# The last row pair: product 2 moved to the end, into a bank that VectorE has seeded with product 1 and the residual

## The chip, the cores and the metric

The kernel runs on one core of one Trainium2 chip. The metric is the device time of one execution in microseconds, the median of several runs. Engines are named as the profile names them: PE (TensorE matmul), PEld (its weight loads), DVE (VectorE), ACT (ScalarE), POOL (GpSimd), SP (the engine that issues most DMAs).

## What is computed

With x of 2048 tokens by 640 channels in float32, and xn its layer norm over the channels, the output is the input plus an FNet mixing sublayer plus a token-mixing MLP:

```python
xn = _layernorm(x)
a, b = xn @ dft_hid_re.T, xn @ dft_hid_im.T
fnet = dft_seq_re @ a - dft_seq_im @ b
u = gelu(h.T @ w1 + b1)          # h = _layernorm(xn); 1728 hidden features per channel
mixer = (u @ w2 + b2).T          # back to 2048 tokens by 640 channels
out = x + fnet + mixer
```

## The kernel before

All large products are computed in float32 accuracy from two reduced pieces of each operand: a high part, made by ScalarE (`high`, L150), and the rest, made by VectorE (`low`, L153). `three` (L158 to L164) multiplies high by high, high by low and low by high, so one 128x128x320 block costs three matmuls (L161, L162, L164).

Each stage is a 2x2 block product done with seven block products in the manner of Strassen and Winograd, called here P1 to P7. `row_steps` (L851) makes one such set for one pair of 128-row output tiles, as seven steps of the program. The stages run one after another: the DFT along the sequence, the one along the channels ("hid"), the two halves of the first MLP matrix ("up0", "up1") and the two halves of the second ("down0", "down1"). The change touches one set alone, the last: stage "down1", t = 7, for which `base` is given. This set writes output rows t and t + 8 for good. All sets before it add their results to `out` in DRAM with accumulating DMAs (`collect`, L1032); the last set instead loads what stands in `out` so far (`before`, L1128: two loads, the residual), adds it on chip, and writes the finished rows with plain DMAs (`each`, L1122).

In this set nq is 3, so the stationary blocks have 384 columns. P1, P5, P6 and P7 take nine matmuls, and P2, P3 and P4 take eight, because the last 64-row block is stacked with its remainder (`stacked`, L918). Four blocks of a weight matrix are loaded (A11, A21, A22, A12). VectorE forms the sums from them: `first_sum` (L866: s = A21 + A22), s2 (L1002: s = s - A11, the operand of P6), s4 (L1004: A12 = A12 - s, the operand of P3) and s3 (L1003: A21 = A11 - A21, the operand of P7). P2 uses A12 as it was loaded, so s4 in place comes after P2's pieces have been cut from A12. `fourth` (L990) has ScalarE repeat 64 rows of the operand of P3.

The products accumulate in four banks of PSUM, called z, y, w and u. P1, P6 and P7 all add into z, and z is read after each of them (P1, then P1 + P6, then P1 + P6 + P7). P5 and P3 add into y, which is read after each. P2 has w to itself, and P4 has u. A fresh bank is the next of eight in turn (`bank`, L168).

`read(i)` (L922) takes the result of product i out of its bank:

- i = 1: ScalarE copies z to the left half of the upper output tile (L962).
- i = 5 and 6: VectorE adds the residual on the way out (L958).
- i = 2, 3, 7: VectorE adds the bank to what stands in the output tile (L949). After 3 it adds the residual to the upper left tile (L975), after 7 it writes z + residual to the lower left tile (L979).
- i = 4, the last: VectorE adds the bank to the lower left tile in two halves of 160 columns (L954), and each half has its own DMA, the first on SP's queue and the second on ScalarE's.

The order on each engine is the program's order. `turn_of` (L1224) writes step i: loads, `read` of the product before, sums, the high piece of step i + 2 (AHEAD is 2), extras, the low piece of step i + 2, then what is listed in `behind_lo`, then the matmuls of step i. So in the turn of P1, the high and low piece of the third product of the set are cut, and behind the low piece stand the sums that `behind_lo[s0]` lists.

Of the kernel before, what the change touches and what calls it, by code (L numbers as in the profile page):

```python
# [14 lines left out]
P = 128  # L15
# [12 lines left out]
H2 = D // 2  # L28
# [49 lines left out]
def fnet_plus_mixer(  # L78
# [30 lines left out]
    nc = tc.nc  # L109
# [741 lines left out]
    def row_steps(stage, nq, load_piece, at, end, bias=(None, None), base=None, earliest=0, each=None, aside={}, tail=False, stacked=()):  # L851
# [27 lines left out]

        order = (1, 5, 2, 6, 3, 7, 4) if base else (1, 5, 6, 2, 7, 3, 4)

        early = n < D
        loads_of = {-6: ("A11", "A21", "A22"), -4: ("A12",)} if early else {
# [13 lines left out]
            new_bank += (7, 3)  # L899
        if base:  # L900
            bank_of[4] = "u"
            new_bank += (4,)
        of_moving = {1: 0, 2: 1, 3: 2, 5: 3, 7: 4, 4: 5, 6: 6}

        goes_to = {1: (0, 0, True), 5: (1, 1, True), 6: (0, 1, True), 2: (0, 0, False), 7: (1, 1, False),
# [16 lines left out]
        def read(i):  # L922
            def run():
                if i == 1:
                    held["c"] = place[at]()
                row, half, fresh = goes_to[i]
                cols = slice(half * H2, (half + 1) * H2)
                c, b = held["c"][:, row, cols], banks[bank_of[i]][:, :H2]
                if tail and i in (5, 7, 4):

                    def upper():
                        aside[i](row, half, b)
                        if i == 4:
                            end(held["c"])


                    if i == 7:
                        upper()
                    else:
                        extras[s0 + (4 if i == 5 else order.index(i) + 1)].append(upper)  # L940
                    if i == 5:
                        nc.scalar.activation(c, b, AF.Copy)
                    else:
                        nc.vector.tensor_add(c[:TAIL], b[:TAIL], c[:TAIL])
                    return
                if i in aside:
                    aside[i](row, half, b)
                elif not fresh:
                    nc.vector.tensor_add(c, b, c)  # L949
                elif base and i == 4:  # L950

                    for k, queue in enumerate((nc.sync, nc.scalar)):
                        of = slice(k * H2 // 2, (k + 1) * H2 // 2)
                        nc.vector.tensor_add(c[:, of], b[:, of], c[:, of])  # L954
                        each(c, row, half, True, of, queue)
                    return
                elif base and i != 1:
                    nc.vector.tensor_add(c, b, base()[:, row, cols])  # L958
                elif bias[row] is not None:
                    nc.scalar.activation(c, b, AF.Identity, bias=bias[row])  # L960
                else:
                    nc.scalar.activation(c, b, AF.Copy)  # L962
                if tail and i == 6:

                    low_row = held["c"][:, 1, :]
                    nc.vector.tensor_add(low_row[:, H2:], b, low_row[:, H2:])
                    extras[s0 + 3].append(lambda: nc.scalar.activation(low_row[:, :H2], b, AF.Copy))
                    p5 = banks["u"][:TAIL, :H2]
                    behind_lo[s0 + 3].append(lambda: nc.vector.tensor_add(c[:TAIL], p5, c[:TAIL]))
                if each:  # L970
                    each(c, row, half, i in (7, 3, 4))
                if base and i == 3:

                    c11 = held["c"][:, 0, :H2]
                    nc.vector.tensor_add(c11, c11, base()[:, 0, :H2])  # L975
                    each(c11, 0, 0, True)
                if base and i == 7:

                    nc.vector.tensor_add(held["c"][:, 1, :H2], b, base()[:, 1, :H2])  # L979
                if i == 4 and not each:  # L980
                    end(held["c"])
            return run

        if stacked:

            def second_time():
                last = raw["s"][:, n - P :]
                nc.scalar.activation(last[TAIL:], last[:TAIL], AF.Copy)

            def fourth():  # L990

                last = raw["A12"][:, n - P :]
                nc.scalar.activation(last[TAIL:], last[:TAIL], AF.Copy)

            if not base:
                extras[s0 + 1].append(second_time)
        for e, names in loads_of.items():
            loads[max(s0 + e, earliest)].append(lambda names=names: load(*names))
        if n == D or stacked:
# [2 lines left out]
            s2 = lambda: sub(raw["s"], raw["s"], raw["A11"])  # L1002
            s3 = lambda: sub(raw["A21"], raw["A11"], raw["A21"])  # L1003
            s4 = lambda: sub(raw["A12"], raw["A12"], raw["s"])  # L1004
            if base:
                sums_of = {-2: (first_sum,)}
                behind_lo[s0 - 1].append(s2)
                behind_lo[s0].extend((s4, s3))
                behind_lo[s0 + 1].append(fourth)
            elif stacked:  # L1010
                sums_of = {-2: (first_sum,), 2: (s4,)}
                behind_lo[s0 - 1].append(s2)
                extras[s0].append(s3)
            elif s0 == s_hid:

                behind_lo[s0 - 2].append(first_sum)
                sums_of = {0: (s2,), 1: (s3,), 2: (s4,)}
            else:
                sums_of = {-2: (first_sum, s3), 2: (s4,)}
                behind_lo[s0 - 1].append(s2)  # L1020
# [283 lines left out]
```

## Time and profile before

| what | value |
|---|---|
| time, median of 3 runs | 866.65 us (866.47 to 866.7) |
| span of the profiled execution (first to last instruction) | 865.1 us |
| PE busy | 860.7 us (99%) |
| DVE busy | 695.2 us (80%) |
| ACT busy | 523.0 us (60%) |
| granted TensorE clock | 1.000 |
| first matmul of the last set (P1) | at 852.96 us |
| last matmul of the program (P4) | starts 861.61 us, 0.31 us long |

The page gives no time of the profiled execution other than its span; the median of the runs is 1.55 us above that span. The timeline lists instructions by their start, with the duration behind it and, in brackets, how long the engine had been idle and what ended that. Durations overlap: a matmul of 128x320 lasts 0.31 us but the next starts 0.147 us later.

### The profile page before, as it was taken

The numbers are of one execution on the slowest core, as the hardware profiler recorded it, in microseconds if no ns is written. First come the engines' busy times: TensorE is split into PE (matmuls) and PEld (weight loads), VectorE is DVE, ScalarE is ACT, GpSimd is POOL, SyncE is SP. The second block draws the span as 40 slices with busy tenths as digits, with TensorE's granted clock in tenths as the row PEclk, the third lists the DMA queues.
The fourth block names the chain that finished last, engine by engine and source line by source line (L and its number), as shares of the span: only waits on it lengthen the run. The fifth ranks groups of instructions, "written<-read, shape, count | busy, mean of one in ns | idle before, by whom it ended". The sixth has DMA issues, their size and how long they took to land.

```text
span 865.1 us, 13904 instructions
## 1 busy us (share of the span) xinstructions
PE 860.7 (99%) x4899; PEld 789.6 (91%) x4899; DVE 695.2 (80%) x1177; ACT 523.0 (60%) x968; POOL 158.8 (18%) x215
## 2 busy tenths in 40 slices
PE   9999999999999999999999999999999999999998
PEld 6888888888888888889999999999999999999998
DVE  7898868758767888677877788888679978987887
ACT  5765576763555555547565556676667866555654
POOL 2222131210020211122110101111312221101211
PEclk9999999999999999999999999999999999999999
DMA  9949596695382746869576766665687689766776
GB/s 337 366 103 268 186 245 235 160 292 151 94 191 29 199 102 135 212 107 200 125 167 157 163 138 196 189 173 162 142 185 176 146 241 244 183 141 126 157 170 149
DMA packets 90293, 154.44 MB, mean 179 GB/s; under 512 B 9008, under 2 KB 37424, under 8 KB 89968
## 3 DMA queue, kind: packets, MB, share of 16 engines
q0 software_dynamic: 25008, 57.52, 36.1%
q1 hardware_dynamic: 64928, 95.80, 34.0%
q8 instruction: 38, 0.62, 0.3%
q10 hardware_dynamic: 288, 0.25, 0.1%
q14 instruction: 31, 0.25, 0.1%
HBM read 99.96 MB, written 58.82 MB: 184 GB/s over the span
## 4 chain that ended last, share of the span: by engine, by line
PE 99%; DMA 1%; SPq 0%; ACT 0%; DVE 0%; issue 0%; DVEq 0%
PE psum L161 32%; PE psum L162 32%; PE psum L164 31%; PE psum L515 3%; DMA pieces<-in_dft_seq 1%; ACT piece L150 0%; SPq L503 0%; SPq L539 0%; DVE pair L954 0%; DVEq L1300 0%
## 5 line engine op out<-in xcount | busy, mean ns | idle before, releaser
L153 DVE TENSOR_TENSOR piece<-pieces,piece 128x512 fp32r<-128x512 f32 (+4 forms) x496 | 327.2, 660 | 129.8 <-ACT piece L150 125.2
L150 ACT ACTIVATE piece<-pieces 128x512 fp32r<-128x512 f32 (+3 forms) x472 | 295.3, 626 | 224.6 <-PE psum L164 143.0
L161 PE MATMUL psum<-piece,n 128*128 128x512 f32 x540 | 210.3, 389 | 0.0
L164 PE MATMUL psum<-piece,n 128*128 128x512 f32 x540 | 210.3, 389 | 0.0
L162 PE MATMUL psum<-piece,n 128*128 128x512 f32 x540 | 210.3, 389 | 0.0
L162 PE MATMUL psum<-sup,piece 128*128 128x320 f32 x392 | 120.9, 309 | 0.0
L162 PE MATMUL psum<-sdown,piece 128*128 128x320 f32 x392 | 120.9, 309 | 0.0
L161 PE MATMUL psum<-sup,piece 128*128 128x320 f32 x392 | 120.9, 309 | 0.0
L161 PE MATMUL psum<-sdown,piece 128*128 128x320 f32 x392 | 120.9, 309 | 0.0
L162 PEld LDWEIGHTS psum<-piece,n 128*128 128x128 f32 x540 | 101.4, 188 | 21.1
L161 PEld LDWEIGHTS psum<-piece,n 128*128 128x128 f32 x540 | 101.4, 188 | 20.9
L164 PEld LDWEIGHTS psum<-piece,n 128*128 128x128 f32 x540 | 101.4, 188 | 20.9
L156 DVE TENSOR_TENSOR pieces<-pieces 128x512 f32<-128x512 f32 (+3 forms) x142 | 111.9, 793 | 3.0
L164 PE MATMUL psum<-sup,piece 128*128 128x320 f32 x368 | 113.9, 310 | 0.0
L164 PE MATMUL psum<-sdown,piece 128*128 128x320 f32 x368 | 113.9, 310 | 0.0
L492 POOL DMA_DIRECT2D y<-c x65 | 56.0, 898 | 255.2 <-DVE c L691 154.0
L164 PE MATMUL psum<-shid,piece 128*128 128x320 f32 x280 | 86.7, 310 | 0.0
L162 PE MATMUL psum<-shid,piece 128*128 128x320 f32 x280 | 86.7, 309 | 0.0
L161 PE MATMUL psum<-shid,piece 128*128 128x320 f32 x280 | 86.6, 309 | 0.0
L161 PEld LDWEIGHTS psum<-sdown,piece 128*128 128x128 f32 x392 | 73.6, 188 | 0.0
L161 PEld LDWEIGHTS psum<-sup,piece 128*128 128x128 f32 x392 | 73.6, 188 | 0.0
L162 PEld LDWEIGHTS psum<-sup,piece 128*128 128x128 f32 x392 | 73.6, 188 | 0.0
(135 smaller groups left out, 1107.2 us busy)
## 6 DMA issues: line engine op xcount, KB each, us to landing
pieces<-in_dft_seq SPq DMA_DIRECT2D x120, 256.0 KB, 5.4
y<-c POOLq DMA_DIRECT2D x105, 256.0 KB, 4.9
pieces<-in_w SPq DMA_DIRECT2D x88, 256.0 KB, 3.8
out<-pair POOLq DMA_DIRECT2D x36, 320.0 KB, 5.5
pieces<-y SPq DMA_DIRECT2D x32, 320.0 KB, 4.2
pieces<-in_w SPq DMA_DIRECT2D x32, 192.0 KB, 2.6
out<-in_x SPq DMA_DIRECT2D x16, 320.0 KB, 8.8
up<-pair POOLq DMA_DIRECT2D x8, 640.0 KB, 3.2
```

The source lines that it names most:

```text
L150: nc.scalar.activation(hi, src, AF.Copy)
L153: nc.vector.tensor_sub(lo, src, hi.bitcast(F32))
L156: nc.vector.tensor_sub(to, a, b)
L161: nc.tensor.matmul(psum, wh, mh, start=first, stop=False, skip_group_check=True)
L162: nc.tensor.matmul(psum, wh, ml, start=False, stop=last and wl is None, skip_group_check=True)
L164: nc.tensor.matmul(psum, wl, mh, start=False, stop=last, skip_group_check=True)
L492: nc.gpsimd.dma_start(y_part[m][c][:, j, :], t, accum_op=ALU.add)
L515: nc.tensor.matmul(banks[m, j], channels(k, j)[rows], w[cols], start=n == 0 and k == begin, stop=n == 2 and k == end, skip_group_check=True,)
```

## The change

Only the set with `base` is changed. The order of its products becomes 1, 5, 6, 3, 7, 4, 2 instead of 1, 5, 2, 6, 3, 7, 4. The read of P1 is no longer a copy by ScalarE to the output tile: VectorE adds bank z and the residual and writes the sum into a fresh bank of PSUM, which becomes w. P2, now the last product, accumulates into w without clearing it. At the end VectorE copies the left 160 columns of w out and ScalarE the right 160; each half goes out with its own DMA, on SP's and ScalarE's queue as before. P4 is read whole, and stored with one DMA. Since A12 must stay as it is until the pieces of P2 are cut, s4 writes to a slot of its own (S4), and `fourth` works on S4.

```diff
-        order = (1, 5, 2, 6, 3, 7, 4) if base else (1, 5, 6, 2, 7, 3, 4)
+        order = (1, 5, 6, 3, 7, 4, 2) if base else (1, 5, 6, 2, 7, 3, 4)
...
         if base:
             bank_of[4] = "u"
-            new_bank += (4,)
+            new_bank = (1, 5, 4)
+            operand[3] = "S4"
...
+                if base and i == 1:
+                    banks["w"] = bank()
+                    nc.vector.tensor_add(banks["w"][:, :H2], b, base()[:, row, cols])
+                    return
+                if base and i == 2:
+                    for k, (queue, copy) in enumerate(((nc.sync, nc.vector.tensor_copy), (nc.scalar, high))):
+                        of = slice(k * H2 // 2, (k + 1) * H2 // 2)
+                        copy(c[:, of], b[:, of])
+                        each(c, row, half, True, of, queue)
+                    return
                 if i in aside:
                     aside[i](row, half, b)
-                elif not fresh:
+                elif not fresh or base and i == 4:
                     nc.vector.tensor_add(c, b, c)
-                elif base and i == 4:
-
-                    for k, queue in enumerate((nc.sync, nc.scalar)):
-                        of = slice(k * H2 // 2, (k + 1) * H2 // 2)
-                        nc.vector.tensor_add(c[:, of], b[:, of], c[:, of])
-                        each(c, row, half, True, of, queue)
-                    return
-                elif base and i != 1:
+                elif base:
                     nc.vector.tensor_add(c, b, base()[:, row, cols])
...
-                if base and i == 3:
-
-                    c11 = held["c"][:, 0, :H2]
-                    nc.vector.tensor_add(c11, c11, base()[:, 0, :H2])
-                    each(c11, 0, 0, True)
...
+            def s4_apart():
+                raw["S4"] = raw_slot(n)
+                sub(raw["S4"], raw["A12"], raw["s"])
+
             if base:
                 sums_of = {-2: (first_sum,)}
                 behind_lo[s0 - 1].append(s2)
-                behind_lo[s0].extend((s4, s3))
-                behind_lo[s0 + 1].append(fourth)
+                behind_lo[s0].extend((s4_apart, fourth, s3))
```

The engines' rows below are the program's order around the two places that change. A name such as psum7_103 is a bank, piece_8205 the pieces of the third product of the set, and the brackets name the engines and DMA queues whose semaphores the row waits for.

First place, VectorE, from the low piece of P5 on, before. The row of L156 behind it is s2, the next two are P2's low piece (in two parts), then come s4 and s3, P6's low piece and the read of P5.

```order
L153 TENSOR_TENSOR piece_8190<-pieces0_123,piece_8190 128x384 [waits Activation_49]
L156 TENSOR_TENSOR pieces0_123<-pieces0_123 128x384 [waits DVE_49]
L153 TENSOR_TENSOR piece_8205<-pieces0_123,piece_8205 64x128 [waits DMAHW2_49,PE_49,Activation_49]
L153 TENSOR_TENSOR piece_8205<-pieces0_123,piece_8205 128x256
L156 TENSOR_TENSOR pieces0_123<-pieces0_123 128x384 [waits DVE_49]
L156 TENSOR_TENSOR pieces0_123<-pieces0_123 128x384
L153 TENSOR_TENSOR piece_8222<-pieces0_123,piece_8222 128x384 [waits PE_49,Activation_49]
L958 TENSOR_TENSOR pair_8220<-psum0_96,pair_8144 128x320 [waits DMASW7_49,DMAHW1_49,DMASW0_49,PE_49]
```

The same place on VectorE after the change: s2, P6's low piece, s4 into its own slot, s3, and then the new add from bank z (psum7_103) into w (psum0_96).

```order
L153 TENSOR_TENSOR piece_8190<-pieces0_123,piece_8190 128x384 [waits Activation_49]
L156 TENSOR_TENSOR pieces0_123<-pieces0_123 128x384 [waits DVE_49]
L153 TENSOR_TENSOR piece_8205<-pieces0_123,piece_8205 128x384 [waits PE_49,Activation_49]
L156 TENSOR_TENSOR pieces0_123<-pieces0_123 128x384 [waits DMAHW2_49]
L156 TENSOR_TENSOR pieces0_123<-pieces0_123 128x384
L949 TENSOR_TENSOR psum0_96<-psum7_103,pair_8144 128x320 [waits DMAHW0_49,PE_49]
L153 TENSOR_TENSOR piece_8222<-pieces0_123,piece_8222 64x128 [waits DVE_49,Activation_49]
L153 TENSOR_TENSOR piece_8222<-pieces0_123,piece_8222 128x256
L962 TENSOR_TENSOR pair_8220<-psum1_97,pair_8144 128x320 [waits DMASW7_49,DMAHW1_49,DMASW0_49,PE_49]
```

The low piece of the third product now needs s2's result, and the read of P1, which VectorE did not do before, stands behind it and behind both sums.

The same place on PE before: the last matmul of P5 and the first of the third product, P2, in a bank of its own.

```order
L164 MATMUL psum0_96<-sdown12_7108,piece_8190 128x320
L161 MATMUL psum1_97<-sdown10_6694,piece_8205 128x320 [waits Activation_49]
L162 MATMUL psum1_97<-sdown10_6694,piece_8205 128x320
L164 MATMUL psum1_97<-sdown10_6694,piece_8205 128x320 [waits DVE_49]
L161 MATMUL psum1_97<-sdown11_6936,piece_8205 128x320
```

And on PE after: the last matmul of P5, and then P6, which adds into P1's bank.

```order
L164 MATMUL psum1_97<-sdown12_7108,piece_8190 128x320
L161 MATMUL psum7_103<-sdown10_6694,piece_8205 128x320 [waits DVE_49,Activation_49]
L162 MATMUL psum7_103<-sdown10_6694,piece_8205 128x320
L164 MATMUL psum7_103<-sdown10_6694,piece_8205 128x320
L161 MATMUL psum7_103<-sdown11_6936,piece_8205 128x320
```

The wait for VectorE has moved from the third matmul of the product to its first.

Second place, the end of the program: ScalarE after the change, from the high piece of P3 on (before, the list ended with the high piece of P4 and the DMA).

```order
L150 ACTIVATE piece_8222<-pieces0_123 128x384 [waits PE_49,Activation_49]
L150 ACTIVATE piece_8236<-pieces0_123 128x384 [waits DVE_49,PE_49]
L150 ACTIVATE piece_8249<-pieces0_123 128x384 [waits DMAHW7_49,PE_49]
L150 ACTIVATE piece_8263<-pieces0_123 128x384 [waits DVE_49,DMAHW2_49,PE_49,Activation_49]
L150 ACTIVATE pair_8220<-psum0_96 128x160 [waits DMASW7_49,DMASW0_49,DVE_49]
L1127 DMA out<-pair_8220 128x160 [waits DMAHW0_49,Activation_49]
```

ScalarE's own half of the last bank is new; it waits for VectorE and for two old DMAs, and names no wait for PE. VectorE's last row is its half.

```order
L960 TENSOR_TENSOR pair_8220<-psum1_97,pair_8220 128x320 [waits DVE_49,PE_49]
L153 TENSOR_TENSOR piece_8263<-pieces0_123,piece_8263 64x128 [waits Activation_49]
L153 TENSOR_TENSOR piece_8263<-pieces0_123,piece_8263 128x256
L960 TENSOR_TENSOR pair_8220<-psum7_103,pair_8220 128x320 [waits PE_49]
L978 TENSOR_TENSOR pair_8220<-psum7_103,pair_8144 128x320
L960 TENSOR_TENSOR pair_8220<-psum2_98,pair_8220 128x320 [waits DVE_49,PE_49]
L954 COPY pair_8220<-psum0_96 128x160 [waits PE_49]
```

Where two adds in a row stood (L954, 128x160 each, both on VectorE), one copy of 128x160 stands on VectorE and one on ScalarE.

More of the change, by code (lines that the diff above doesn't have):

```diff
@@ L990, in fourth @@
             def fourth():
-                last = raw["A12"][:, n - P :]
+                last = raw["S4" if base else "A12"][:, n - P :]
                 nc.scalar.activation(last[TAIL:], last[:TAIL], AF.Copy)
```

## The prediction

> **What bounds the kernel now.** I read the page's busy times and its chain of work first, since they say whether any engine but PE matters.
>
> ```profile
> span 865.1 us, 13904 instructions
> PE   860.7 (99%) x4899; PEld 789.6 (91%) x4899; DVE 695.2 (80%) x1177; ACT 523.0 (60%) x968; POOL 158.8 (18%) x215
> PE 99%; DMA 1%; SPq 0%; ACT 0%; DVE 0%; issue 0%; DVEq 0%
> ```
>
> PE is the chain from the first microseconds to the last. The change leaves every matmul before the last set alone and neither adds nor drops one in it (P1 to P7 are 60 before and after). So its effect has two parts only: a gap that it opens or closes between matmuls of the last set, and the path behind the last matmul. Next I read the timeline of that set, PE alone: the last two matmuls of P5, the first of the product behind it, and the last two of the program.
>
> ```profile
> 855.30 0.31 PE L162 MATMUL psum<-sdown,piece 128*128 128x320 f32 x1
> 855.45 0.31 PE L164 MATMUL psum<-sdown,piece 128*128 128x320 f32 x1
> 855.60 0.31 PE L161 MATMUL psum<-sdown,piece 128*128 128x320 f32 x1
> ...
> 861.47 0.31 PE L161 MATMUL psum<-sdown,piece 128*128 128x320 f32 x1
> 861.61 0.31 PE L162 MATMUL psum<-sdown,piece 128*128 128x320 f32 x1
> ```
>
> The third product starts one ordinary step of 0.147 us behind the second: no gap. 41 steps lie between 855.60 and 861.61, at 0.147 each, so there is no gap later either. Before the change, the set is bound by PE's rate alone; there is no stall to win back. The last matmul ends at 861.92.
>
> **The first part: who now releases the third product.** It is P6 instead of P2. P2 had a bank of its own; P6 adds into P1's bank, so it must not start until P1 has been read. Before, ScalarE read P1, at once and two products ahead of P6. Now VectorE reads it, and the order shows where: behind s2, the low piece of P6, s4 and s3. That P6's first matmul waits for this very add follows from the waits: the third matmul needs the low piece and names no wait any more, so the wait on VectorE at the first reaches further than the low piece, and the add is the only reader of psum7_103 there. What VectorE and ScalarE do around this point before:
>
> ```profile
> 853.69 0.56 DVE L156 TENSOR_TENSOR pieces<-pieces 128x384 f32<-128x384 f32 x1
> 854.28 0.73 DVE L153 TENSOR_TENSOR piece<-pieces,piece 64x128 fp32r<-64x128 f32 x2
> 854.48 0.44 ACT L962 ACTIVATE pair<-psum 128x320 f32<-128x320 f32 x1 [0.47 <-PE psum L164]
> 855.04 1.03 DVE L156 TENSOR_TENSOR pieces<-pieces 128x384 f32<-128x384 f32 x2
> 855.63 0.31 ACT L993 ACTIVATE pieces<-pieces 64x128 f32<-64x128 f32 x1 [0.30 <-DVE pieces L156]
> 855.97 0.53 ACT L150 ACTIVATE piece<-pieces 128x384 fp32r<-128x384 f32 x1
> 855.99 0.55 DVE L153 TENSOR_TENSOR piece<-pieces,piece 128x384 fp32r<-128x384 f32 x1
> 856.45 0.48 DVE L958 TENSOR_TENSOR pair<-psum,pair 128x320 f32<-128x320 f32 x1
> ```
>
> ScalarE had emptied P1's bank at 854.92. VectorE starts s2 at 853.69; nothing ahead of s2 changes, so that holds after the change as well. What follows is new in this set, but the set before it (t = 6) has exactly this chain, s2, then ScalarE's high piece of P6, then VectorE's low piece:
>
> ```profile
> 844.89 1.03 DVE L156 TENSOR_TENSOR pieces<-pieces 128x384 f32<-128x384 f32 x2
> 845.54 0.53 ACT L150 ACTIVATE piece<-pieces 128x384 fp32r<-128x384 f32 x1 [0.74 <-DVE pieces L156]
> 846.10 0.56 DVE L153 TENSOR_TENSOR piece<-pieces,piece 128x384 fp32r<-128x384 f32 x1 [0.18 <-ACT piece L150]
> ```
>
> From the start of s2 to the start of the low piece are 1.21 us. So the low piece of P6 starts at 853.69 + 1.21 = 854.90. Back to back, 384-column operations follow each other every 0.47 us (two L156 and the next L153: 855.04 to 855.99; L153 to L958: 0.46). So s4 starts at 855.37, s3 at 855.84, and the new add at 856.31. The trace has no VectorE operation that writes PSUM. The nearest rows are the same add with its output in SBUF, 0.48 (L958 above), and from below the 0.40 after which VectorE itself goes on (L949 at 857.61, next row 858.01, quoted further down); from above I double it, 0.97. I take 0.48, the row with the same sources and size: the add ends at 856.79.
>
> Then PE has to be woken. The only waits of PE for another engine lie at the start of the kernel:
>
> ```profile
> 6.54 0.63 ACT L150 ACTIVATE piece<-pieces 128x512 fp32r<-128x512 f32 x1 [1.57 <-DMA pieces<-in_dft_seq]
> 7.23 0.73 PE L515 MATMUL psum<-piece,n 128*128 128x512 f32 x2 [0.27 <-ACT piece L150]
> 7.23 2.12 PE L515 MATMUL psum<-piece,n 128*128 128x512 f32 x8 [0.27 <-ACT piece L150]
> ```
>
> ScalarE ends at 7.17 and PE starts at 7.23: 0.06. The first two matmuls take 0.73, all eight 2.12, so six further steps take 1.39, or 0.23 each, while the first step takes 0.73 - 0.39 = 0.34 (one matmul of that width is 0.39 long): 0.11 more, the weight load that nothing hides. P6 then runs as if its first matmul had started at 856.79 + 0.06 + 0.11 = 856.96, not 855.60: **1.36 us**. P6 waits for two semaphores, one of them in an instruction ahead of the matmul, for which I add 0.04: **1.4 us** lost. From below 1.3 (the add released 0.08 earlier), from above 1.9 (a doubled add).
>
> Is the loss given back or repeated? It can't be given back: behind P6 PE runs at its rate, and 42 matmuls remain. Repeated it could be at P3, which adds into P5's bank and waits for VectorE's read of P5. S4 starts at 855.37; from s4 to the end of the high piece of its product is 1.46 (855.04 to 856.50 above, with L993 between), so ScalarE is done at 856.83 and the two-part low piece starts at 856.86. The rows below show that the next add follows 0.64 later: 857.50 to 857.98. P3 is due at 856.96 + 9 x 0.147 = 858.28. So 0.24 us is spare, after a handoff of 0.06. P7 waits for VectorE's read of P6, which can't begin before P6's last matmul has ended (856.96 + 8 x 0.147 + 0.31 = 858.45) and ends near 859.0; P7 is due at 859.45. P4 and P2 have banks of their own, and their pieces have 0.6 us and more to spare, since the gap lets ScalarE and VectorE catch up. Nothing further is late.
>
> ```profile
> 856.97 0.73 DVE L153 TENSOR_TENSOR piece<-pieces,piece 64x128 fp32r<-64x128 f32 x2
> 857.61 0.48 DVE L949 TENSOR_TENSOR pair<-psum,pair 128x320 f32<-128x320 f32 x1
> 858.01 0.55 DVE L153 TENSOR_TENSOR piece<-pieces,piece 128x384 fp32r<-128x384 f32 x1
> ...
> 860.04 0.48 DVE L975 TENSOR_TENSOR pair<-pair 128x320 f32<-128x320 f32 x1
> ...
> 861.19 0.48 DVE L979 TENSOR_TENSOR pair<-psum,pair 128x320 f32<-128x320 f32 x1
> 861.96 0.56 DVE L954 TENSOR_TENSOR pair<-psum,pair 128x160 f32<-128x160 f32 x2 [0.28 <-PE psum L162]
> 862.55 0.35 ACTq L1124 DMA_DIRECT2D out<-pair  x1
> ```
>
> Costs at nothing: the residual is now wanted at 856.31 instead of 858.48, but its loads were issued at 843.25 and landed 4.8 us later at most:
>
> ```profile
> 843.25 0.84 SPq L1132 DMA_DIRECT2D pair<-out  x2
> DMA to landing us min/median/max: 4.5/4.6/4.8
> ```
>
> The add L975 goes (0.48 on VectorE); it stood beside matmuls, so it is worth nothing. P4's store becomes one DMA, issued when VectorE has read P4, eight matmuls ahead of the end. Before, the store of the tile read after P7 stood at the same distance (L949 at 860.79, P4 behind it also has eight), so SP's queue is as far ahead of the last store as it was.
>
> **The second part: behind the last matmul.** Before, both adds of 160 columns run on VectorE: start at 861.96, 0.04 behind PE's end; the second ends at 862.52, and the DMA of its half, the last, is issued at 862.55, or 0.63 behind PE's end. The change wants the halves side by side. The order says otherwise: ScalarE's copy names no wait for PE, although PE has just filled the bank. It waits for VectorE, and the only row of VectorE that itself waits for the last matmul is the other half's copy. So the halves go one behind the other, now with a handoff between two engines.
>
> ```profile
> L954 DVE TENSOR_TENSOR pair<-psum,pair 128x160 f32<-128x160 f32 x2 | 0.6, 320 | 0.3 <-PE psum L162 0.3
> L878 DVE COPY pieces<-pieces 64x128 f32<-64x128 f32 x8 | 1.8, 224 | 0.3
> L962 ACT ACTIVATE pair<-psum 128x320 f32<-128x320 f32 x97 | 42.2, 435 | 43.8 <-PE psum L164 40.7 <-PE psum L162 2.2
> L988 ACT ACTIVATE pieces<-pieces 64x128 f32<-64x128 f32 x7 | 2.2, 309 | 0.2
> ```
>
> VectorE's copy lies between the small copy, 0.22, and the add of the same size, 0.32; I take 0.29, nearer the add, whose size it has. The handoff to ScalarE is 0.03 (855.04 + 0.56 to 855.63). ScalarE's copy lies between 0.44 (320 columns) and, for 128 columns, 0.31: I take 0.31, the nearer in size, and its DMA follows 0.03 later. So the last DMA goes out at 0.04 + 0.29 + 0.03 + 0.31 + 0.03 = 0.70 behind PE's end instead of 0.63: **0.07 us later** (0.00 to 0.23 by the bounds). What lies behind that DMA is the same transfer and the same end of the program.
>
> The Trainium skill has the rule behind this wait: "PSUM — Partial Sum Buffer", section "PSUM bank collisions raise a hardware error", says that two engines must not access the same bank and quadrant at once, reads against reads included, and that software has to order them. The order's wait agrees; by the rule the halves can't overlap, and without it ScalarE's half would end as early as VectorE's and the term would be about -0.3.
>
> **Sum.** +1.4 + 0.07 = +1.47 us on a span of 865.1, so 866.6. The page has no other time of that execution; the median of the runs is 1.55 above the span, and I add the difference to the median: 866.65 + 1.47 = **868.1 us**, 0.17% slower. A measurement of this kernel can tell about 0.2% (1.73 us) from no change, so this counts as within 0.2%.
>
> **Rivals.**
>
> *A dearer seed.* If the add into PSUM takes longer than the one into SBUF, each tenth goes straight into PE's gap. From +0.26 on, the total passes 1.73 and the change is slower by over 0.2%; with the doubled add it is 866.65 + 1.9 + 0.07 = 868.6. For it: no row shows a write to PSUM. Against it: reading PSUM costs nothing (L979 reads PSUM, L975 reads SBUF alone, 0.48 both).
>
> *The gap costs the clock.* The clock row shows that PE's clock does fall behind its work:
>
> ```profile
> 863.60:864.60 1.00, 0.00 (x0) 0.00 (x0) 0.00 (x0) 0.00 (x0) 0.00 (x0) 1.00 0.14 39
> 864.60:865.10 0.50, 0.00 (x0) 0.00 (x0) 0.00 (x0) 0.00 (x0) 0.00 (x0) 0.53 0.00 0
> ```
>
> The clock (behind the engines' columns) is full up to 864.60, 2.7 us after the last matmul, and 0.53 in the half microsecond behind it. Were the 42 remaining matmuls to run at half, they'd take 6.2 us more: 874.3. My gap is 1.1 us of idle (855.76 to 856.89), less than half of 2.7, so the trace speaks against it. The Trainium skill, "TensorE: Matmul & The Clock Gate", Part 1, has the clock halve after an idle window of about 3.4 us; by that rule, too, this gap is short of it.
>
> *No stall.* If the release of P6 came by 855.60 (the add done 1.3 us earlier than I have it, as when it stood ahead of the low piece in VectorE's row), only the tail would count: 866.65 + 0.07 = 866.7, and with a tail as the change describes it (halves side by side, ScalarE's DMA at 0.04 + 0.31 + 0.03 = 0.38 instead of 0.63) 866.4. That is the other side, faster than before; it decides at an add that ends before 855.5, and VectorE's order, which is fixed, speaks against it. *Halves side by side with the stall* gives 866.65 + 1.4 - 0.25 = 867.8: the change does at the end what it says. The wait in ScalarE's row speaks against it.
>
> **How the numbers follow.** Forecast 0.77 (868.1; 867.9 to 868.35 by its bounds without the doubled add); dearer seed or a second wait at P3 0.13 (868.4 to 868.8); halves side by side 0.04; no stall 0.04; clock 0.02. The range of 867.6 to 868.7 takes in the first three cases. Faster by over 0.2% would need 1.73 us, and the best case above, no stall with the halves side by side, gains 0.25; so 0.02 for what I don't see. Slower by over 0.2%: the dearer seed, the clock and a little of the forecast's upper edge, 0.17. Within 0.2%: 0.81.
>
> **What would show it.** PE's timeline should have one gap, between the end of P5 and a first matmul of P6 near 856.9, released by VectorE's add (L949 of the new kernel) that starts near 856.3; no gap at P3 or P7; the last matmul 1.4 us later relative to the start, and ScalarE's copy of 160 columns starting after VectorE's has ended, not beside it. The prediction is wrong if P6 follows P5 without a gap, if the add's row is not near 0.48, if P3 shows a gap of its own, or if both copies start together.

## The result, and the profile after

The changed kernel takes **868.23 us** (median of 16 runs, 868.1 to 869.73) against 866.65 for the kernel before (16 runs, 866.38 to 868.49). The ratio is 1.0019, 95% interval 1.0012 to 1.0026: 0.19% slower, where 868.1 was forecast. The profiled span grew from 865.1 to 866.5 us.

First the busy times of the page of the kernel after. They say almost nothing: PE still works 860.6 us.

```profile
span 866.5 us, 13903 instructions
PE 860.6 (99%) x4899; PEld 789.3 (91%) x4899; DVE 694.7 (80%) x1176; ACT 522.8 (60%) x968; POOL 158.8 (18%) x215
```

The place shows in PE's timeline of the last set: the last matmul of P5, the first two of P6, and the last one of the program.

```profile
855.23 0.31 PE L164 MATMUL psum<-sdown,piece 128*128 128x320 f32 x1
856.73 0.38 PE L161 MATMUL psum<-sdown,piece 128*128 128x320 f32 x1 [1.19 <-ACT piece L150]
856.95 0.31 PE L162 MATMUL psum<-sdown,piece 128*128 128x320 f32 x1
...
862.81 0.31 PE L162 MATMUL psum<-sdown,piece 128*128 128x320 f32 x1
```

P6 starts 1.495 us behind the last matmul of P5 instead of 0.147, and its second matmul 0.22 behind its first. All other steps are ordinary, so PE loses 1.42 us in all, at this one place. The whole set began 0.22 us earlier in this execution than in the one of before (P1 at 852.74 instead of 852.96); such an offset is not the change's, so from here on times are compared by their distance to P1's start or to PE's end.

VectorE and ScalarE at the same place, from s2 to the read of P5:

```profile
853.47 0.56 DVE L156 TENSOR_TENSOR pieces<-pieces 128x384 f32<-128x384 f32 x1
854.12 0.52 ACT L150 ACTIVATE piece<-pieces 128x384 fp32r<-128x384 f32 x1 [0.74 <-DVE pieces L156]
854.68 0.56 DVE L153 TENSOR_TENSOR piece<-pieces,piece 128x384 fp32r<-128x384 f32 x1 [0.65 <-ACT piece L150]
855.15 1.02 DVE L156 TENSOR_TENSOR pieces<-pieces 128x384 f32<-128x384 f32 x2
855.74 0.31 ACT L992 ACTIVATE pieces<-pieces 64x128 f32<-64x128 f32 x1 [1.09 <-DVE pieces L156]
856.08 0.94 ACT L150 ACTIVATE piece<-pieces 128x384 fp32r<-128x384 f32 x2
856.09 0.49 DVE L949 TENSOR_TENSOR psum<-psum,pair 128x320 f32<-128x320 f32 x1
856.64 0.73 DVE L153 TENSOR_TENSOR piece<-pieces,piece 64x128 fp32r<-64x128 f32 x2
857.28 0.48 DVE L962 TENSOR_TENSOR pair<-psum,pair 128x320 f32<-128x320 f32 x1
```

L949 is the new add: it starts 2.62 us behind s2, ends at 856.58, and P6 follows 0.15 later. The view of waits, which lists who waited for whom, how long and how often, names another releaser:

```profile
PE psum L161 <- ACT piece L150: 1.2, 1, 1.2
```

This is a wait put down to the wrong engine. The L150 that ends at 856.61 (856.08 + 0.52) is the high piece of **P3**, nine matmuls further on. P6 waits on ScalarE for its own high piece, and that was done at 854.64. The first experiment shows which reading is right.

The end of the program after: VectorE's copy, ScalarE's copy, the last DMA.

```profile
863.16 0.33 DVE L954 COPY pair<-psum 128x160 f32<-128x160 f32 x1 [0.68 <-PE psum L162]
863.52 0.30 ACT L150 ACTIVATE pair<-psum 128x160 f32<-128x160 f32 x1 [3.45 <-DVE pair L954]
863.85 0.35 ACTq L1127 DMA_DIRECT2D out<-pair  x1
```

The copies stand one behind the other, 0.03 apart. PE's end is where its last matmul ends (862.81 + 0.31 = 863.12). The last DMA is issued 0.73 us behind it, before 0.62; the span ends 3.39 behind PE's end, before 3.17. So the change costs 1.42 on PE and 0.22 behind it, 1.64 together, of which the medians show 1.58.

### The profile page after: what moved, and what is told of

It reads as the page before. It is cut to its first block, busy times and chain, and to the rows that moved or that the text cites. A ratio compares the mean times of both kernels' runs of the same rounds, so it can differ in the third digit from the quotient of the medians.

```text
span 866.5 us, 13903 instructions
## 1 busy us (share of the span) xinstructions
PE 860.6 (99%) x4899; PEld 789.3 (91%) x4899; DVE 694.7 (80%) x1176; ACT 522.8 (60%) x968; POOL 158.8 (18%) x215
## 4 chain that ended last, share of the span: by engine, by line
PE 98%; DVE 1%; DMA 0%; ACT 0%; issue 0%; SPq 0%; ACTq 0%
PE psum L161 32%; PE psum L162 32%; PE psum L164 31%; PE psum L515 3%; DMA pieces<-in_dft_seq 0%; DVE piece L153 0%; ACT piece L150 0%; DVE pair L960 0%; DVE pieces L156 0%; DVE pieces L874 0%; SPq L539 0%; DVE n L394 0%; DVE pair L954 0%; ACT pieces L992 0%; ACT near L236 0%
## 5 line engine op out<-in xcount | busy, mean ns | idle before, releaser
L150 ACT ACTIVATE piece<-pieces 128x512 fp32r<-128x512 f32 (+3 forms) x472 | 295.3, 626 | 225.2 <-PE psum L164 140.4
L156 DVE TENSOR_TENSOR pieces<-pieces 128x512 f32<-128x512 f32 (+3 forms) x142 | 111.7, 792 | 3.4 <-DMA pieces<-in_dft_seq 0.5
L161 PEld LDWEIGHTS psum<-sdown,piece 128*128 128x128 f32 x392 | 73.6, 188 | 1.4 <-ACT piece L150 1.4
L161 PEld LDWEIGHTS psum<-sup,piece 128*128 128x128 f32 x392 | 73.6, 188 | 0.0
L162 PEld LDWEIGHTS psum<-sdown,piece 128*128 128x128 f32 x392 | 73.6, 188 | 0.0
```

The lines of the kernel that those rows point to most:

```text
L150: nc.scalar.activation(hi, src, AF.Copy)
L156: nc.vector.tensor_sub(to, a, b)
L161: nc.tensor.matmul(psum, wh, mh, start=first, stop=False, skip_group_check=True)
L162: nc.tensor.matmul(psum, wh, ml, start=False, stop=last and wl is None, skip_group_check=True)
```

## The experiments

That PE waits at P6 is seen; what has to be told apart is why. The first theory, called A where the expectations use letters, is that of the **cover**: P2 needs no sum, so in third place its eight matmuls (1.17 us) hid the chain by which VectorE and ScalarE get P6 and P3 ready. Without P2 there, something of that chain is late whatever the details, and curing one link shows the next. Against it stand the edits themselves: that VectorE reads P1, late in its queue; that the sum is written into PSUM; and, at the end, the handoff between two engines. Line numbers differ by a few between kernels. "PE loss" is what the 60 matmuls of the set take beyond 0.147 us a step.

### VectorE reads P1 before it cuts P6's low piece

```diff
+        if i == len(steps) - 7:
+            def low_later():
+                ready[j] = steps[j][1]()
+            sums[i + 1].extend([low_later] + behind_lo.pop(i))
-        if 0 <= j < len(steps):
+        elif 0 <= j < len(steps):
             ready[j] = steps[j][1]()
```

> The changed kernel with VectorE's read of P1 moved ahead of the low piece of P6, so that it stands directly behind s2. Theory A (the loss is cover, not one row): PE's gap in front of P6 goes, but with P2 no longer between P6 and P3, P3 comes due about 1.32 us behind the start of P6, and its chain on VectorE (s4, s3, low piece of P3, read of P5) is as late as before; so the gap moves to P3, 1.2 to 1.35 us long, and the time stays near 868.05 (1.39 us above the kernel before). Theory B (the place of the read of P1 in VectorE's row is the whole cause): no gap anywhere, 866.75, the tail's 0.1 us above the kernel before.

Measured: 868.19 us, ratio 1.002 (1.0011 to 1.0029). In this kernel, VectorE's read of P1, then ScalarE's high pieces from P3's on, and VectorE's low piece of P3 and read of P5:

```profile
854.30 0.50 DVE L949 TENSOR_TENSOR psum<-psum,pair 128x320 f32<-128x320 f32 x1 [0.23 <-PE psum L164]
...
856.13 1.35 ACT L150 ACTIVATE piece<-pieces 128x384 fp32r<-128x384 f32 x3
856.69 0.73 DVE L153 TENSOR_TENSOR piece<-pieces,piece 64x128 fp32r<-64x128 f32 x2 [0.47 <-ACT piece L150]
857.33 0.48 DVE L962 TENSOR_TENSOR pair<-psum,pair 128x320 f32<-128x320 f32 x1
```

Its PE: the end of P5 and the start of P6, then the end of P6 and the start of P3.

```profile
855.28 0.31 PE L164 MATMUL psum<-sdown,piece 128*128 128x320 f32 x1
855.42 0.31 PE L161 MATMUL psum<-sdown,piece 128*128 128x320 f32 x1
...
856.60 0.31 PE L164 MATMUL psum<-sdown,piece 128*128 128x320 f32 x1
857.96 0.38 PE L161 MATMUL psum<-sdown,piece 128*128 128x320 f32 x1 [1.06 <-DVE pair L962]
```

P6 has no gap now, although P3's high piece, the first of the three in the row of L150, ends no earlier than in the kernel after (856.13 + 0.52 = 856.65, or 3.87 behind P1's start in both): so it was VectorE's add that P6 waited for, and the wait view was wrong. But the gap has only moved. P3 adds into P5's bank, whose read stands behind P3's own low piece, and it loses 1.29. In the kernel after this second wait was hidden behind the first with 0.21 to spare (the read ends at 857.76, P3 may start 0.15 later, and was due at 858.12): 1.42 less 0.21 is 1.21, and with the 0.07 of P3's slow second step 1.28.

### The product order alone

The order of the products and S4 stay, and all else is as before the change: ScalarE copies P1, P2 has a bank of its own, VectorE adds at the end.

```diff
-            new_bank = (1, 5, 4)
+            new_bank = (1, 5, 2, 4)
...
-                    banks["w"] = bank()
-                    nc.vector.tensor_add(banks["w"][:, :H2], b, base()[:, row, cols])
+                    nc.scalar.activation(c, b, AF.Copy)
...
-                        copy(c[:, of], b[:, of])
+                        nc.vector.tensor_add(c[:, of], b[:, of], c[:, of])
...
+                if base and i == 3:
+                    c11 = held["c"][:, 0, :H2]
+                    nc.vector.tensor_add(c11, c11, base()[:, 0, :H2])
```

> The changed kernel's product order and its S4 slot, but P1 is read by ScalarE to the output tile as before the change, P2 has a bank of its own, nothing is seeded in PSUM, and the last product is added out in two halves on VectorE as before. Theory A (cover): no gap at P6, a gap of 1.2 to 1.35 us at P3, tail as before the change; 867.9 to 868.0. Theory B (the read of P1 on VectorE is the cause): no gap, 866.65. Theory C (writing the seed to PSUM is what costs): no gap, 866.65.

Measured: 868.21 us, 1.0019 (1.0009 to 1.0028). The loss on PE is 1.63: 1.32 at P6 and 0.31 at P3. No theory had the first. ScalarE shows why, from the repeat of 64 rows (`fourth`) to its read of P1, and PE at P6:

```profile
855.66 0.31 ACT L994 ACTIVATE pieces<-pieces 64x128 f32<-64x128 f32 x1 [1.09 <-DVE pieces L156]
856.03 0.44 ACT L948 ACTIVATE pair<-psum 128x320 f32<-128x320 f32 x1
```

```profile
855.16 0.31 PE L164 MATMUL psum<-sdown,piece 128*128 128x320 f32 x1
856.52 0.41 PE L161 MATMUL psum<-sdown,piece 128*128 128x320 f32 x1 [1.05 <-ACT pair L948]
```

`fourth` now stands in the turn of P1 and waits for s4, and ScalarE's read of P1 is queued behind it. So this kernel had a new obstacle of its own, and didn't yet show what the order costs. The same edit with `fourth` one turn later:

```diff
+        if i == len(steps) - 7:
+            sums[i + 1].append(behind_lo[i].pop(1))
```

> The kernel of order_alone, with ScalarE's repeat of the 64 rows of S4 moved behind its read of P1, since it had stood ahead of it and waited for s4. Theory A (cover): no gap at P6; P3 is held by the chain s4, repeat, high piece, low piece, read of P5, which nothing in this kernel shortens, so one gap of 1.2 to 1.35 us at P3, tail as before the change (last DMA 0.62 us behind PE's end), 867.9 to 868.1. Theory B (VectorE's read of P1): no gap, 866.65.

Measured: 867.92 us, 1.0015 (1.0006 to 1.0024), with a loss of 1.27, all at P3. VectorE's read of P5, then PE at the end of P6 and the start of P3:

```profile
857.26 0.48 DVE L961 TENSOR_TENSOR pair<-psum,pair 128x320 f32<-128x320 f32 x1
856.54 0.31 PE L164 MATMUL psum<-sdown,piece 128*128 128x320 f32 x1
857.89 0.39 PE L161 MATMUL psum<-sdown,piece 128*128 128x320 f32 x1 [1.04 <-DVE pair L961]
```

This kernel has no seed in PSUM, ScalarE reads P1 in good time, and its tail is that of before (0.62 and 3.17 behind PE's end, as there). It is still 1.32 slower. So the order of the products, with VectorE's queue left as it is, is enough to bring the cost: by way of s4, `fourth`, the high and the low piece of P3 and the read of P5. The seed is not needed for it.

### The end of the program on VectorE alone

```diff
-                    for k, (queue, copy) in enumerate(((nc.sync, nc.vector.tensor_copy), (nc.scalar, high))):
+                    for k, (queue, copy) in enumerate(((nc.sync, nc.vector.tensor_copy), (nc.scalar, nc.vector.tensor_copy))):
```

> The changed kernel with both halves of the last bank copied by VectorE, one behind the other, each with its own DMA as now. If ScalarE's half waits for VectorE's half and the handoff and ScalarE's longer start are what the tail pays, the last DMA is issued 0.62 us behind PE's end instead of 0.73 and the time falls by 0.10 us, to about 868.13; the gap at P6 stays at 1.4 us. If the two engines side by side were worth something, it would rise by 0.1 or more.

Measured: 868.09 us, 1.0017 (1.0008 to 1.0026). The two copies and the last DMA of this kernel, whose PE ends at 863.18:

```profile
863.22 0.55 DVE L954 COPY pair<-psum 128x160 f32<-128x160 f32 x2 [0.68 <-PE psum L162]
863.80 0.35 ACTq L1127 DMA_DIRECT2D out<-pair  x1
```

Two copies take 0.55, two adds took 0.56 before. So a copy out of PSUM is no cheaper than an add with PSUM, and the seed, which turns the last add into a copy, buys nothing. The DMA goes out 0.62 behind PE's end, as before. Handing the second half to ScalarE costs 0.11 there, and 0.13 more until the span's end (3.15 here, 3.39 in the kernel after). The medians, 0.14 apart, have overlapping intervals; the profile carries this reading.

### VectorE's queue in another order

VectorE does s2, s4, the read of P1, P6's low piece, s3, the read of P5, P3's low piece: each read ahead of the low piece that stood in its way, and s3 one turn later.

```diff
+        at = i - (len(steps) - 7)
+        if 0 <= at < 3:
+            def low_later():
+                ready[j] = steps[j][1]()
+            sums[i + 1].append(low_later)
+            if at == 0:
+                sums[i + 1].append(behind_lo[i].pop())
-        if 0 <= j < len(steps):
+        elif 0 <= j < len(steps):
             ready[j] = steps[j][1]()
```

> The changed kernel with VectorE's rows rearranged in the last set: s2, s4, read of P1, low piece of P6, s3, read of P5, low piece of P3, read of P6, low piece of P7. Theory A (cover): every release now comes at or just before PE needs it; a gap of 0.0 to 0.25 us is left at P3's third matmul, which waits for the low piece, and the time is 866.75 to 867.0. If the gap came from the seed in PSUM or from the product order as such, it would stay near 1.4 us and 868.2.

Measured: 867.14 us, 1.0005 (0.9997 to 1.0014). VectorE's reads of P1 and P5 and P3's low piece:

```profile
854.58 0.49 DVE L949 TENSOR_TENSOR psum<-psum,pair 128x320 f32<-128x320 f32 x1
...
855.92 0.48 DVE L962 TENSOR_TENSOR pair<-psum,pair 128x320 f32<-128x320 f32 x1
856.43 0.73 DVE L153 TENSOR_TENSOR piece<-pieces,piece 64x128 fp32r<-64x128 f32 x2
```

And PE at the second and third matmul of P3:

```profile
856.88 0.31 PE L162 MATMUL psum<-sdown,piece 128*128 128x320 f32 x1
857.22 0.41 PE L164 MATMUL psum<-sdown,piece 128*128 128x320 f32 x1
```

Both banks come free in time. What is left is the low piece of P3, which ends at 857.16, so that the third matmul of P3 waits: 0.28 us of loss instead of 1.42. The seed is still there, and so is the handoff at the end. It is therefore VectorE's queue that sets how much of the cover is missed. The time is 0.14 above the expected range: the gap is 0.03 longer than its upper bound, and the tail, counted at 0.1, costs 0.21.

### The last bank in one copy, or in two banks

Both build on the kernel above. In the first ScalarE copies all 320 columns, then both DMAs go out. In the second the halves of P2 have banks of their own, so that the two copies may run side by side; its 8 matmuls become 16 of 160 columns.

```diff
-                    for k, (queue, copy) in enumerate(((nc.sync, nc.vector.tensor_copy), (nc.scalar, high))):
+                    high(c, b)
+                    for k, queue in enumerate((nc.sync, nc.scalar)):
                         of = slice(k * H2 // 2, (k + 1) * H2 // 2)
-                        copy(c[:, of], b[:, of])
```

> The kernel of vector_order, with the last bank copied out by one ScalarE operation of 320 columns, and the two half DMAs behind it. The copy should take 0.44 us and both DMAs go out 0.50 to 0.56 us behind PE's end, instead of 0.39 and 0.73; the gap at P3 stays at 0.28. If the later of the two DMAs sets the end, the time falls by 0.15 to 0.2 us against vector_order, to 866.95; if the earlier one counts, it rises by 0.1.

```diff
+                    if base and i == 2:
+                        for k in range(2):
+                            of = slice(k * H2 // 2, (k + 1) * H2 // 2)
+                            three(
+                                banks["w"][k][:, of], (w[0][:, ks], None if q == nq - 1 else w[1][:, ks]),
+                                (m[:, 0, of_moving[i], of], m[:, 1, of_moving[i], of]), False, q == nq - 1,
+                            )
+                        continue
...
-                        copy(c[:, of], b[:, of])
+                        copy(c[:, of], banks["w"][k][:, of])
```

> The kernel of vector_order, with P2 accumulated in two banks, 160 columns each (16 matmuls of 160 columns instead of 8 of 320), seeded by two adds. If the shared bank is what puts ScalarE's half behind VectorE's, both copies now start together, 0.04 us behind PE's end, and the last DMA goes out at 0.40 instead of 0.73. If something else orders them, ScalarE still starts 0.36 later. The 16 matmuls take 1.2 us at best (no more than 8 of 320) and 2.3 us if their pace is that of 320 columns. Time 866.9 to 867.3, or 868 at that worst pace.

One copy: 867.18 us, 1.0007 (0.9998 to 1.0016), no better than two. The copy itself is quick:

```profile
861.98 0.44 ACT L150 ACTIVATE pair<-psum 128x320 f32<-128x320 f32 x1 [3.09 <-PE psum L162]
862.45 0.37 ACTq L1127 DMA_DIRECT2D out<-pair  x1
```

Both DMAs go out 0.50 behind PE's end (861.94), 0.23 ahead of the last one in the kernel above, yet the span ends 3.44 behind PE instead of 3.38. The expected gain is lost behind the issue: the first packet of ScalarE's DMA starts 1.02 us after it instead of 0.87, and SP comes to its last wait 2.44 behind PE's end instead of 2.38. In this execution the two transfers, started together, were slower than two that are 0.34 apart.

Two banks: 867.41 us, 1.001 (1.0001 to 1.0018). One of P2's matmuls, and the copies at the end:

```profile
862.01 0.28 PE L161 MATMUL psum<-sdown,piece 128*128 128x160 f32 x1
862.13 0.27 PE L162 MATMUL psum<-sdown,piece 128*128 128x160 f32 x1
862.21 0.32 DVE L965 COPY pair<-psum 128x160 f32<-128x160 f32 x1 [1.03 <-PE psum L162]
862.44 0.30 ACT L150 ACTIVATE pair<-psum 128x160 f32<-128x160 f32 x1 [3.67 <-PE psum L162]
862.77 0.35 ACTq L1138 DMA_DIRECT2D out<-pair  x1
```

Here the halves do overlap, from 862.44 to 862.53, each as long as alone, and the last DMA goes out 0.37 behind PE's end (862.40). ScalarE's copy now waits for PE and no longer for VectorE. The Trainium skill, "PSUM — Partial Sum Buffer", section "Specifications (TRN2)", says that ScalarE and VectorE reach PSUM in parallel at full rate as long as they don't meet in a bank; these rows agree. The price is on PE: a matmul of half the columns comes every 0.112 us, not every 0.073. From its first matmul (860.49) to PE's end the product takes 1.91 us instead of 1.34. It earns 0.36 at the last DMA against 0.57 on PE, and the time lies 0.11 above the range expected at the better paces.

### s3 on GpSimd

The kernel with VectorE's queue in another order again, with the sum s3 taken off VectorE.

```diff
+            def s3_pool():
+                nc.gpsimd.tensor_sub(raw["A21"], raw["A11"], raw["A21"])
...
-                behind_lo[s0].extend((s4_apart, fourth, s3))
+                behind_lo[s0].extend((s4_apart, fourth, s3_pool))
```

> The kernel of vector_order, with s3 computed by GpSimd, which is idle here, so that VectorE has 0.47 us less to do ahead of the read of P5. Theory A (VectorE's queue sets every release): the gap of 0.28 us at P3 goes (0.00 to 0.1), the time is 866.7 to 866.9, the tail's 0.1 above the kernel before. If GpSimd's sum is late for P7 (more than 2 us long), a gap appears there instead.

Measured: 866.96 us, 1.0005 (0.9996 to 1.0014). The PE loss is 0.11, still at the third matmul of P3. The time is 0.06 above the expected range, again for the tail of 0.22 that was counted at 0.1. P6's low piece on VectorE, GpSimd's sum, and P3's low piece:

```profile
854.80 0.55 DVE L153 TENSOR_TENSOR piece<-pieces,piece 128x384 fp32r<-128x384 f32 x1
854.93 1.30 POOL L1006 TENSOR_TENSOR pieces<-pieces 128x384 f32<-128x384 f32 x1
855.97 0.85 DVE L153 TENSOR_TENSOR piece<-pieces,piece 64x128 fp32r<-64x128 f32 x2
```

P3's low piece takes 0.85 instead of 0.73 while GpSimd works beside it, which is most of what is left. With the tail on VectorE as well (the edit of the third experiment on top):

> The kernel of pool_sum with the tail of tail_vector: both cures together. If gap and tail simply add, the gap at P3 stays near 0.11 us, the span behind PE's end falls from 3.39 to 3.15 us, and the time is 866.6 + 0.1 = 866.65 to 866.8, level with the kernel before. If P2 at the end with a seeded bank has a gain of its own, the time falls below 866.5.

Measured: 866.71 us against 866.64, ratio 1.0001 (0.9992 to 1.001), the loss on PE 0.13, the span's end 3.16 behind PE. The cost of the change is gone, and nothing is gained over the kernel before. The last try puts GpSimd's sum two products earlier, where the expectation had it harmless:

```diff
-                sums_of = {-2: (first_sum,)}
+                sums_of = {-2: (first_sum,), -1: (s3_pool,)}
...
-                behind_lo[s0].extend((s4_apart, fourth, s3_pool))
+                behind_lo[s0].extend((s4_apart, fourth))
```

> As pool_vector_tail, with GpSimd's sum issued one step earlier, ahead of its two stores, so that it runs beside other work of VectorE than the low piece of P3. In pool_sum that low piece took 0.85 us instead of 0.73 while GpSimd's sum ran. If that overlap is the 0.11 us that is left at P3, the gap goes to 0.00 to 0.05 and the time is 866.55 to 866.7; if not, it stays at 0.11 and 866.7. No gain below 866.5 is expected either way, since the copies at the end take as long as the adds did.

Measured: 867.08 us, 1.0005 (0.9996 to 1.0014): a miss, with a PE loss of 0.40, of which 0.30 at P6. VectorE's last low piece before P5's, GpSimd's sum, and VectorE from P5's low piece on:

```profile
852.04 0.56 DVE L153 TENSOR_TENSOR piece<-pieces,piece 128x384 fp32r<-128x384 f32 x1
852.15 1.33 POOL L1006 TENSOR_TENSOR pieces<-pieces 128x384 f32<-128x384 f32 x1 [5.92 <-DVE pieces L878]
852.92 0.98 DVE L153 TENSOR_TENSOR piece<-pieces,piece 128x384 fp32r<-128x384 f32 x1
853.93 1.15 DVE L156 TENSOR_TENSOR pieces<-pieces 128x384 f32<-128x384 f32 x2
```

The low piece of P5 now runs beside the sum and takes 0.98 instead of 0.55; s2 and everything behind it start 0.43 later. The Trainium skill, "SBUF — State Buffer", section "Who interferes with whom", says that a VectorE instruction with two inputs in SBUF and a GpSimd instruction that reads SBUF hold a shared port exclusively, the later one blocked until the other is done. The rows agree: GpSimd's sum ends at 853.48, and the low piece ends 0.42 behind that, about the 0.47 that such an operation occupies VectorE. They agree the other way round too: in both kernels the sum starts about 0.1 behind a low piece of VectorE, and it ends 0.88 behind that piece's end (852.60 to 853.48 here, 855.35 to 856.23 in the first kernel with GpSimd). By the rule, 0.42 to 0.45 of its 1.3 us would be waiting; no run has the sum by itself. By that rule the place of GpSimd's sum has to be one where VectorE reads PSUM or waits, and this chain has little of it.

### All runs together

Each row: time, change of the median against the kernel before on the same chip, PE loss, change of the span's end behind PE, and the sum of the two.

| kernel | time us | change | PE loss | end | sum |
|---|---|---|---|---|---|
| the change | 868.23 | +1.58 | 1.42 (P6) | +0.22 | 1.64 |
| read of P1 first | 868.19 | +1.56 | 1.29 (P3) | +0.21 | 1.50 |
| order alone | 868.21 | +1.58 | 1.63 (P6, P3) | 0.00 | 1.63 |
| order alone, `fourth` later | 867.92 | +1.32 | 1.27 (P3) | 0.00 | 1.27 |
| tail on VectorE | 868.09 | +1.46 | 1.43 (P6) | -0.02 | 1.41 |
| VectorE's queue | 867.14 | +0.51 | 0.28 (P3) | +0.21 | 0.49 |
| one copy | 867.18 | +0.58 | 0.27 (P3) | +0.27 | 0.54 |
| s3 on GpSimd | 866.96 | +0.36 | 0.11 (P3) | +0.22 | 0.33 |
| s3 on GpSimd, tail on VectorE | 866.71 | +0.07 | 0.13 (P3) | -0.01 | 0.12 |
| GpSimd's sum early | 867.08 | +0.44 | 0.40 (P6) | +0.01 | 0.41 |

Two banks stands apart, since its last product has other matmuls: 867.41, +0.81. In every row the two terms give the change to within 0.06 us. That is what lets differences of 0.3 us be read that no interval of the ratios resolves.

## Why the prediction was right, point by point

**The release of P6** held, term by term. The add starts 2.62 us behind s2, exactly as forecast (856.31 less 853.69). It takes 0.49, forecast 0.48: writing PSUM costs nothing over writing SBUF, and the doubled add of the rival is out. PE starts 0.15 behind the add's end instead of 0.10 (of which 0.04 rested on no row), and the slow first step, put down to the exposed weight load, costs 0.07 instead of 0.11: 0.22 for 0.21. That these two cancel is luck. Together 1.42, forecast 1.4.

**No gap at P3** held: 0.21 us was spare, forecast 0.24. But the prediction took this as the end of the matter, and the experiments show that it is half of the cause. The prediction named the place of the add in VectorE's queue as the reason, and its rival without a stall let the loss vanish if the add stood ahead of P6's low piece. That rival's price was wrong: with the add there the kernel is still 1.56 slower, because P3 has a chain of nearly the same length behind it. What costs is that P2, the one product that needs no sum, no longer stands in third place while VectorE's queue stays as it was: with that queue in another order the loss is 0.28, with P2 still last.

**The clock** stayed full through the gap, as said. The margin was smaller than the prediction's 2.7 us, though: in the kernel with two banks the clock had fallen 1.6 us behind the last matmul (last section). The window from 855.70 to 857.10 of the kernel after; the clock stands behind the five engines' columns:

```profile
855.70:857.10 1.40, 0.37 (x3) 0.40 (x3) 1.33 (x5) 1.24 (x3) 0.00 (x0) 1.00 1.21 181
```

**The tail** was right in kind, the halves one behind the other, and short in size: +0.22 where +0.07 was forecast. VectorE's copy took 0.325 instead of 0.29; the nearer row, the add of the same size, was the right one to the last digit, and going below it was the error. ScalarE's copy took 0.30 (forecast 0.31), the handoff 0.03. So the last DMA is 0.105 later, not 0.07. The other 0.12 is behind that DMA, where "the same end of the program" was assumed: from SP's last wait to the end of the span are 1.01 us, before 0.89. In all kernels whose last copy is ScalarE's this stretch is 1.00 to 1.01, and 0.87 to 0.89 in all where VectorE does it. One drain of SP is longer by 0.10; the first row is the kernel after, the second the kernel before (least, median and longest time in ns).

```profile
L1303 SPq DRAIN  x3: 7/7/118, 865.6 to 866.2; - x3
```

```profile
L1300 SPq DRAIN  x3: 7/7/18, 864.3 to 864.8; - x3
```

Why the end of the program depends on who copied last stays open; the runs show only that the two go together. Also open is what the halves would give if they ran side by side in one bank: wherever both engines copied out of one bank here, ScalarE's half waited for VectorE's, so no run shows it.

**The range.** The measured 868.23 lies within the forecast's own bounds of 867.9 to 868.35. The upper one is not the sum of its terms, which is 868.28 (866.65 + 1.4 + 0.23); the terms as measured, 1.42 and 0.22, give 868.29.

## What to carry to other kernels

When a product, a tile or a step is moved, ask what its old place was hiding: here 1.17 us of matmuls that needed no sum covered a chain of sums and pieces on two slower engines, and the profile of before, without any gap, could show that only through who was due when. Curing the first late link isn't a cure until the next one is checked: P6 alone was late by 1.42 us and P3 alone by 1.29, so an experiment on one of them by itself would have shown nothing. And behind the last matmul, price a copy out of PSUM as the add that it replaces, and count a second engine as a second step in line unless it has a bank of its own.

## What the runs showed of the hardware beyond that

- PE follows the engine that it waits for at different distances. The first matmul of a product came 0.15 us behind the end of a VectorE read in the kernel after (856.58 to 856.73), with the read first (857.81 to 857.96) and with the order alone and `fourth` later (857.74 to 857.89), but 0.05 behind ScalarE's read (856.47 to 856.52). The third matmul of P3, whose bank and high piece were ready, came 0.06 behind VectorE's low piece (857.16 to 857.22). So it isn't the engine alone that sets the distance; what does stays open.
- The clock does not fall a fixed time behind the last matmul. Before, it had dropped 2.7 us behind it. After, it is still full in the window that ends 2.9 us behind PE's end:

```profile
865.10:866.00 0.90, 0.00 (x0) 0.00 (x0) 0.00 (x0) 0.00 (x0) 0.00 (x0) 1.00 0.00 0
```

With two banks it was at 0.51 from 864.00 to 864.50, that is from 1.6 us behind PE's end (862.40) on. There, and in the kernel before, PE had idled for less than the window of about 3.4 us that the prediction cites from the Trainium skill, so the measurement decides.

- The wait view can name an engine that had nothing to do with a wait: of an instruction that waits for two engines it gave the event that lay closest in time, though it belonged to a later product.
